# Transposes of a fused linear-attention and rational-activation MLP kernel by DMA instead of TensorE, with the queues, the stores, the start and the end rearranged

## The chip, the cores and the metric

The kernel runs on one core of a Trainium2 chip. The metric is the device time of one execution in microseconds (us), the median of several. The engines are named PE (TensorE matrix products) and PEld (its weight loads), DVE (VectorE), ACT (ScalarE), POOL (GpSimd) and SP (SyncE, which here only issues DMAs). Accumulators of TensorE lie in PSUM, everything else on the chip in SBUF. 16 DMA engines move data for all queues.

## The reference

```python
# attention: q, k, v, f_logit have shape (4, 8, 768, 48): batch, heads, time, head dimension
f = 1.0 / (1.0 + np.exp(-f_logit))
for t in range(S):
    state = f[:, :, t, :, None] * state + np.einsum('bhd,bhe->bhde', k[:, :, t], v[:, :, t])
    y[:, :, t] = np.einsum('bhd,bhde->bhe', q[:, :, t], state)
x = y.transpose(0, 2, 1, 3).reshape(3072, 384)
# MLP with a rational activation: w_in is (384, 2048), w_out (2048, 384)
h = x @ w_in
P = a[0] + a[1] * h + a[2] * h2 + a[3] * h3
Q = 1.0 + np.abs(b[0]) * np.abs(h) + np.abs(b[1]) * h2
return (P / (Q + 1e-06)) @ w_out
```

## The kernel before

The 3072 tokens are cut into 12 units of 256. A unit is loaded (`fn`, `kn`, `qn`, `vn`), its decays are summed and exponentiated (`cs`, `A0`, `A1`), multiplied into q and k (`qkp`), and transposed (`qkT`), because the scores `sc` contract over the head dimension. Masked scores and states give `y`, which ACT copies to `xT`. Each unit then has two groups of the MLP (24 groups in all): first-layer products `hp`, the numerator in `t`, the denominator's polynomial in `z`, a logarithm and an exponential (`lq`, `qi`) in place of a division, `gall = t * qi`, and the output products. The order of all instructions is fixed by a list of 654 tokens such as `T:4` (transposes of unit 4) or `Ub:11` (polynomial sum of group 23).

```python
def a_T(n, ps=ALL):                       # 16 transposes on TensorE, into PSUM
    ...
    for b in range(UB):
        for i in range(2):
            for p in range(npairs(ps)):
                nc.tensor.transpose(tp[:, b, i, p, :], s["qk"][:, i, ps.start + p, b].rearrange("t i d -> t (i d)"), ident)

def a_Te(n, ps=ALL):                      # and the copy out of PSUM, on ACT or VectorE
    copy(te_engine(n), t.rearrange(...), s["tp", 0].rearrange(...))

def m_add_u(n):                           # z += h: a DMA that adds, in GpSimd's queue, or VectorE
    ...
    if n in U_BY_DMA:
        nc.gpsimd.dma_start(out=s["u"], in_=s["h2"], accum_op=ALU.add)
    else:
        nc.vector.tensor_add(s["u"], s["z"], s["h2"])

def m_oe(m, b, eng, queue=None):          # copy of an output tile, and at once its store in SP's queue
    ...
    copy(eng, osb, ops.pop((m, b)))
    ...
    (queue or nc.sync).dma_start(out=dst[:, b, :], in_=osb)

# in the loop over the tokens: once unit n has read its inputs, those of unit n + 3 are loaded (SP's queue)
        if key in ("efl", "mq", "mk"):
            read[n] = read.get(n, 0) + 1
            if read[n] == 3 and n + 3 < NUN:
                load(n + 3)
```

Of the kernel before, what the change touches and what calls it, by code (L numbers as in the profile page):

```python
# [18 lines left out]
    efl-:0 efl:0 cs-:0 A0-:0 A1-:0 cs:0 A1:0 mk-:0 A0:0 mq-:0 T-:0 mk:0 mq:0 Te-:0 T:0 sc0:0 sv:0 Te:0  # L19
    efl:1 m0:0 al:0 sc1:0 st:0 cs:1 A0:1 m1:0 y-:0 mq:1 y:0 A1:1 mk:1 sw:0 su:0 xe:0 T:1 Te:1 ha0:0  # L20
    Ya0:0 ha1:0 sc0:1 sv:1 m0:1 Ya1:0 vl:3 al:1 st:1 sc1:1 za:0 efl:2 qa:0 cs:2 A1:2 ta:0 Ua:0 m1:1 sa:0
    hb0:0 sw:1 Ba:0 y:1 mk:2 A0:2 hb1:0 La0:0 Pa:0 Yb0:0 Ea:0 su:1 xe:1 mq:2 Yb1:0 T:2 ga:0 ha1:1 Te:2
    Ya1:1 ha0:1 zb:0 qb:0 Ya0:1 tb:0 Ub:0 Lb0:0 sc0:2 m0:2 Bb:0 hb0:1 sv:2 Ba:1 sc1:2 hb1:1 al:2 za:1
    m1:2 oa0:0 st:2 sw:2 Yb0:1 Eb:0 y:2 Yb1:1 qa:1 efl:3 sb:0 cs:3 xe:2 tb:1 A1:3 ta:1 Pb:0 ha1:2 A0:3
    zb:1 Ya1:2 gb:0 mq:3 ha0:2 Ya0:2 su:2 efl:4 qb:1 Bb:1 hb1:2 Yb1:2 oa1:0 Ua:1 Oa:0 cs:4 mk:3 T:3 Ub:1
    ta:2 La0:1 ob0:0 ob1:0 sa:1 sv:3 vl:4 Te:3 A1:4 sc0:3 qa:2 Ea:1 Ob:0 A0:4 efl:5 hb0:2 mk:4 m0:3
    sc1:3 mq:4 al:3 vl:5 m1:3 cs:5 st:3 sw:3 Lb0:1 sb:1 A0:5 y:3 za:2 Yb0:2 Pb:1 ua1:2 A1:5 qb:2 xe:3
    Eb:1 ua0:2 La1:2 su:3 T:4 sv:4 Pa:1 zb:2 La0:2 ga:1 Ub:2 ha0:3 Te:4 Ba:2 al:4 ha1:3 sc0:4 tb:2 mk:5
    gb:1 m0:4 Ya0:3 sa:2 efl:6 st:4 mq:5 vl:6 oa0:1 Bb:2 Ya1:3 Ea:2 oa1:1 sc1:4 hb1:3 sb:2 m1:4 sw:4
    Yb1:3 hb0:3 Oa:1 cs:6 Yb0:3 ob0:1 A0:6 y:4 za:3 qb:3 Pa:2 A1:6 ob1:1 qa:3 Lb0:2 ta:3 xe:4 su:4 T:5  # L30
    ha0:4 sa:3 zb:3 sv:5 Pb:2 Ba:3 ha1:4 ga:2 tb:3 Eb:2 Bb:3 Te:5 Ob:1 sc0:5 oa0:2 Ya0:4 efl:7 Ua:3 gb:2
    m0:5 mq:6 Ub:3 al:5 Pa:3 st:5 Ya1:4 oa1:2 Oa:2 hb0:4 sc1:5 La0:3 mk:6 Yb0:4 ob0:2 Ea:3 sw:5 sb:3
    vl:7 m1:5 hb1:4 ta:4 Yb1:4 cs:7 Lb0:3 qa:4 za:4 y:5 Ua:4 ob1:2 Ba:4 xe:5 T:6 sa:4 qb:4 zb:4 A1:7
    ha1:5 A0:7 su:5 sv:6 mq:7 Te:6 sc0:6 Pb:3 Ya1:5 Ob:2 ga:3 m0:6 Ub:4 ha0:5 sc1:6 al:6 st:6 Eb:3 oa0:3
    La0:4 hb0:5 Ya0:5 tb:4 m1:6 y:6 Ea:4 Pa:4 vl:8 sb:4 Bb:4 gb:3 za:5 sw:6 xe:6 mk:7 qa:5 oa1:3 Yb0:5
    Oa:3 hb1:5 ta:5 su:6 Ba:5 sa:5 T:7 Te:7 sv:7 ha1:6 efl:8 Yb1:5 ga:4 al:7 Lb0:4 Ya1:6 tb:5 cs:8 A0:8
    sc0:7 ob0:3 st:7 ob1:3 m0:7 zb:5 A1:8 ua1:5 sc1:7 Pb:4 sw:7 qb:5 m1:7 Eb:4 La1:5 ha0:6 gb:4 Ya0:6
    ua0:5 Ob:3 y:7 hb1:6 mq:8 efl:9 Bb:5 sb:5 mk:8 La0:5 xe:7 Pa:5 cs:9 Yb1:6 A0:9 T:8 Ub:5 ta:6 za:6
    oa0:4 Ea:5 Ba:6 qa:6 su:7 hb0:6 oa1:4 Te:8 A1:9 Yb0:6 ha1:7 sa:6 Lb0:5 ga:5 vl:9 ha0:7 Ya1:7 Oa:4
    sc0:8 Pb:5 tb:6 zb:6 sv:8 qb:6 ob0:4 m0:8 Pa:6 ua1:6 Ya0:7 al:8 Eb:5 mk:9 ua0:6 La1:6 st:8 La0:6  # L40
    sc1:8 ob1:4 sb:6 Bb:6 m1:8 Ba:7 za:7 sv:9 Ub:6 efl:10 hb0:7 Ea:6 y:8 hb1:7 Yb0:7 xe:8 gb:5 mq:9 Pb:6
    ha0:8 vl:10 Ob:4 qa:7 al:9 T:9 ta:7 Ua:7 Yb1:7 st:9 Bb:7 Lb0:6 ha1:8 Ya0:8 oa0:5 qb:7 Ya1:8 Te:9
    zb:7 oa1:5 Eb:6 Oa:5 cs:10 efl:11 ga:6 A0:10 A1:10 sa:7 sc0:9 Pa:7 hb0:8 tb:7 ob0:5 m0:9 sc1:9 gb:6
    ta:8 Yb0:8 mq:10 m1:9 ob1:5 hb1:8 La0:7 ub1:7 Ba:8 mk:10 qa:8 Yb1:8 y:9 Ob:5 za:8 Ea:7 Lb1:7 sb:7
    xe:9 vl:11 ga:7 ub0:7 tb:8 Lb0:7 Ua:8 zb:8 oa0:6 qb:8 cs:11 A1:11 T:10 A0:11 Pb:7 Te:10 Eb:7 Ub:8
    oa1:6 ha1:9 Oa:6 sa:8 sv:10 sc0:10 al:10 ha0:9 La0:8 st:10 mk:11 m0:10 Ya1:9 ob0:6 Ya0:9 Ea:8 ob1:6
    sc1:10 Pa:8 Lb0:8 sb:8 hb1:9 Bb:8 Ob:6 m1:10 hb0:9 Yb0:9 za:9 qa:9 sv:11 y:10 gb:7 ta:9 Yb1:9 xe:10
    mq:11 Ba:9 Eb:8 oa0:7 qb:9 Pb:8 al:11 T:11 Ua:9 zb:9 sa:9 Te:11 oa1:7 ga:8 ha0:10 Oa:7 sc0:11 tb:9
    La0:9 Ub:9 ha1:10 st:11 ob0:7 m0:11 sc1:11 Ya1:10 Ya0:10 Pa:9 Bb:9 ob1:7 Ea:9 sb:9 m1:11 hb0:10 Ob:7
    Lb0:9 hb1:10 za:10 qa:10 y:11 gb:8 Pb:9 Ua:10 Yb0:10 oa0:8 oa1:8 ta:10 Yb1:10 Ba:10 xe:11 Eb:9 Oa:8  # L50
    La0:10 sa:10 ha0:11 ha1:11 zb:10 qb:10 ob0:8 ga:9 Pa:10 Ub:10 tb:10 ob1:8 Bb:10 Ya0:11 sb:10 Ya1:11
    Pb:10 Ea:10 gb:9 za:11 hb1:11 Ob:8 Yb1:11 hb0:11 qa:11 Yb0:11 ta:11 Ba:11 oa0:9 sa:11 Ua:11 Lb0:10
    oa1:9 qb:11 zb:11 Oa:9 ob0:9 ga:10 tb:11 Ub:11 Eb:10 La0:11 ob1:9 Ea:11 Pa:11 Ob:9 gb:10 Lb0:11
    ob0:10 oa0:10 sb:11 Bb:11 ob1:10 Eb:11 ga:11 oa1:10 Oa:10 oa0:11 Pb:11 ob0:11 gb:11 ob1:11 oa1:11
    Oa:11 Ob:10 Ob:11
# [3 lines left out]
P_BY_DMA = {4, 5, 6, 7, 8, 9, 10, 11, 12, 13, 14, 15, 16, 17, 18, 19, 20, 21}  # L59

U_BY_DMA = {2, 3, 5, 6, 7, 8, 9, 11, 13, 14, 16, 17, 18, 19, 20, 21, 22, 23}

TE_ON_ACT = {1, 2, 4, 5, 6, 11}
O_ON_DVE = {(0, 1), (11, 1), (10, 1), (2, 0), (9, 1)}
# [3 lines left out]
def kernel(  # L68
# [74 lines left out]
    hold = w_pool.tile([1, 4, 16], BF16, name="hold")  # L143
# [6 lines left out]
    NUN = len(units)  # L150
    at_ = {}
# [3 lines left out]
    def load(n):  # L155
        c, u = units[n]
        at_[n] = dict(qk=qkp[n % NQK], ls=lsp[n % NQK], st=states[u], c=c, u=u)
        for name, src in (("fn", f_logit), ("kn", k), ("qn", q)):
            at_[n][name] = ld.tile([C, H, UB, D], F32, name=name)
            if n > 0:  # L160
                nc.sync.dma_start(out=at_[n][name].rearrange("p h b d -> p h (b d)"), in_=rows(src, n))
        if n == 0:
            for ps in HALVES:
                for name, src in (("fn", f_logit), ("kn", k), ("qn", q)):
                    for i in range(2):
                        hs = slice(HP * i + ps.start, HP * i + ps.stop)
                        nc.sync.dma_start(out=at_[n][name][:, hs].rearrange("t h b d -> t h (b d)"),
                                          in_=rows(src, n)[:, hs])

    def load_v(n):  # L170
        at_[n]["vn"] = vz[n % NV]
        for cc in range(UB):
            w = slice(CH * cc, CH * cc + CH)
            nc.gpsimd.dma_start(out=vz[n % NV][w, :, cc].rearrange("p h b d -> p h (b d)"), in_=rows(v, n)[w])  # L174

# [59 lines left out]
    def a_T(n, ps=ALL):  # L235

        s = at_[n]
        pool, tag = (psr, "r") if ps is HALVES[1] else (psA, "A")
        tp = pool.tile([P, UB, 2, npairs(ps), C], BF16, name="tp", tag=tag)
        for b in range(UB):  # L240
            for i in range(2):
                for p in range(npairs(ps)):
                    nc.tensor.transpose(tp[:, b, i, p, :],  # L243
                                        s["qk"][:, i, ps.start + p, b].rearrange("t i d -> t (i d)"),
                                        ident)
        s["tp", ps.start] = tp

# [3 lines left out]
    def a_Te(n, ps=ALL):  # L251
        s = at_[n]
        t = tile_at(s, "qkT", [P, UB, 2, HP, C], BF16)
        if ps is ALL:
            copy(te_engine(n), t.rearrange("p j a b c -> p (j a b c)"),
                 s["tp", 0].rearrange("p j a b c -> p (j a b c)"))
        else:
            copy(te_engine(n), t[:, :, :, ps].rearrange("p j a b c -> p (j a) (b c)"),
                 s["tp", ps.start].rearrange("p j a b c -> p (j a) (b c)"))
# [29 lines left out]
    def a_sc(n, half):  # L289
# [3 lines left out]
        for q_ in range(2):  # L293
            p = half * 2 + q_
            for b in range(UB):
                for i in range(2):
                    for cc in range(UB):
                        r, w = slice(64 * i, 64 * i + D), slice(CH * cc, CH * cc + CH)
                        nc.tensor.matmul(sc[w, i, q_, b, :], s["qkT"][r, b, 1, p, w], qcols(s, r, p, w),  # L299
# [7 lines left out]
    def qcols(s, r, p, w):  # L307
        return s["qkT"][r, :, 0, p, w]
# [10 lines left out]
    def a_y(n, ps=ALL):  # L319
# [7 lines left out]
        def clear(kk, r):  # L327
# [28 lines left out]
        if ps.start == 0:  # L356
            for kk in (0, KD - 1):
                clear(kk, slice(0, P))
        product(True, [(1, 1)])
        product(False, [(1, 1)])  # L360
        for i in range(2):
            if ps.start == 0:
                clear(0, slice(64 * i + 32, 64 * i + 48))
            if ps.stop == HP:
                clear(KD - 1, slice(64 * i, 64 * i + 16))
# [46 lines left out]

    def m_y(n, half):
        nc.scalar.copy(part_of(tile_of(n, "y"), half), mg[n]["hp", half].rearrange("p a n -> p (a n)"))  # L414

    def m_sq(n):
        s = mg[n]
        s["h2"] = ms.tile([P, W], BF16, name="h2")
        nc.vector.tensor_mul(s["h2"], s["y"], s["y"])  # L419

    def m_abs(n):
        s = mg[n]
        s["z"] = ms.tile([P, W], BF16, name="z")
        nc.vector.tensor_scalar(s["z"].bitcast(U16), s["y"].bitcast(U16), 0x7FFF, None,  # L424
# [21 lines left out]
    def m_ln(n, half):  # L446
        s = mg[n]
        lq = tile_of(n, "lq", F32, bufs=1)
        whole = "u" in s
        nc.scalar.activation(lq if whole else part_of(lq, half),  # L450
                             s["u"] if whole else s["u", half].rearrange("p a n -> p (a n)"),
                             AF.Ln, scale=sig[:, 2:3], bias=1.0 + 1e-6)
# [5 lines left out]

    def m_t(n):
# [211 lines left out]
```

## Time and profile before

| what | before |
|---|---|
| median time | 233.1 us at first, 233.3 beside the changed kernel, 233.5 in the later rounds |
| span in the profile | 231.3 us |
| copies into `xT` start at | 20.72 us (unit 0), then 35.84, 48.99, 68.59 ... 197.16 (unit 11) |
| last `xT` to the end | 34.1 us |

### The profile page before, as it was taken

What the parts mean: (1) busy time and instruction counts of PE and PEld (TensorE: products, weight loads), DVE (VectorE), ACT (ScalarE), POOL (GpSimd) and SP (SyncE); (2) the same over time, 40 slices, a digit from 0 to 9 for tenths busy, and PEclk for the clock granted to TensorE, in tenths of its full rate; (3) what the DMA queues carried; (4) which work ended last, traced back from release to release, by engine and by line L of the source; (5) the groups of instructions that cost most, each with busy time, mean ns of one, the idle gap of its engine ahead of it and who ended that gap; (6) DMA issues with size and microseconds to landing.
All of it is one profiled execution on the core that took longest, in us unless ns stands there. A gap on an engine that the chain in (4) does not pass through costs nothing.

```text
span 231.3 us, 7110 instructions
## 1 busy us (share of the span) xinstructions
PE 211.0 (91%) x3106; PEld 150.1 (65%) x3106; DVE 212.1 (92%) x257; ACT 202.1 (87%) x202; POOL 66.3 (29%) x91
## 2 busy tenths in 40 slices
PE   7299797979989999999999999999999999997981
PEld 3166565767657767676776775876677878764540
DVE  5686599999999999999999999999999999999950
ACT  4424889997999999999999999999998999799950
POOL 8360860023305126035112411424132122313000
PEclk9959979999979999999999999999999999999998
DMA  7999999999999999999999999876599969998502
GB/s 108 261 144 202 186 188 199 222 250 258 197 272 262 187 222 206 183 272 194 185 202 247 192 261 203 131 140 125 74 181 212 203 120 205 188 213 198 127 34 102
DMA packets 63054, 43.71 MB, mean 189 GB/s; under 512 B 51760, under 2 KB 58416, under 8 KB 63024
## 3 DMA queue, kind: packets, MB, share of 16 engines
q0 software_dynamic: 21632, 24.38, 65.9%
q1 hardware_dynamic: 41104, 18.88, 32.7%
q8 instruction: 24, 0.39, 0.7%
q10 hardware_dynamic: 288, 0.00, 0.1%
q14 instruction: 6, 0.05, 0.1%
HBM read 25.17 MB, written 4.72 MB: 129 GB/s over the span
## 4 chain that ended last, share of the span: by engine, by line
DVE 58%; PE 21%; issue 10%; DMA 6%; ACT 3%; SPq 1%; POOL 0%; DVEq 0%; POOLq 0%; ACTq 0%
DVE scm L315 8%; DVE h L419 8%; DVE gall L485 8%; DVE t L465 7%; PE op L502 7%; PE hp L400 6%; DVE t L460 5%; DVE qkp L232 5%; DVE pb L468 5%; DVE z L424 4%; DVE qkT L249 2%; PE y L352 2%; DMA z<-h 2%; DVE t L476 2%; DVE state L381 2%
## 5 line engine op out<-in xcount | busy, mean ns | idle before, releaser
L400 PE MATMUL hp<-xT,w_in_sb 128*128 128x256 bf16 x576 | 70.2, 275 | 0.6 <-ACT y L414 0.2
L502 PE MATMUL op<-w_out_sb,gall 128*128 128x384 bf16 x368 | 65.5, 326 | 2.4 <-ACT osb L249 1.7
L400 PEld LDWEIGHTS <-w_in_sb 128*128 128x128 bf16 x576 | 55.1, 99 | 11.1 <-issue 2.0
L502 PEld LDWEIGHTS <-gall 128*128 128x128 bf16 x384 | 36.1, 98 | 26.4 <-issue 2.2
L414 ACT CAST y<-hp 128x1024 bf16<-128x1024 f32 x48 | 48.0, 1024 | 1.7 <-PE hp L400 0.9
L455 ACT ACTIVATE qi<-lq 128x2048 bf16<-128x2048 f32 x24 | 46.4, 1934 | 0.1
L450 ACT ACTIVATE lq<-z,sig 128x2048 f32<-128x2048 bf16 x20 | 40.4, 2020 | 2.9 <-DMA z<-h 2.8
L442 POOL DMA_DIRECT2D z<-h x18 | 17.1, 949 | 88.5 <-DVE z L424 38.4
L315 DVE TENSOR_TENSOR scm<-sc,mask 128x1024 bf16<-128x1024 f32 x24 | 29.1, 1213 | 4.2 <-PE sc L299 4.2
L474 POOL DMA_DIRECT2D t<-pb x18 | 17.5, 975 | 45.7 <-DVE t L465 30.1
L485 DVE TENSOR_TENSOR gall<-t,qi 128x2048 bf16<-128x2048 bf16 x24 | 29.1, 1211 | 1.0 <-ACT qi L455 1.0
L465 DVE TENSOR_TENSOR t<-t,h 128x2048 bf16<-128x2048 bf16 x24 | 29.1, 1211 | 0.0
L419 DVE TENSOR_TENSOR h<-y 128x2048 bf16<-128x2048 bf16 x24 | 29.0, 1211 | 0.0
L226 ACT ACTIVATE A<-cs 128x768 f32<-128x768 f32 (+1 forms) x26 | 18.7, 767 | 4.2 <-PE cs L217 4.1
L174 POOL DMA_DIRECT2D vz<-in_v_dram x24 | 21.8, 1131 | 0.3 <-POOL vz L531 0.3
L460 DVE TENSOR_SCALAR t<-y,a_sb 128x2048 bf16<-128x2048 bf16 x24 | 19.4, 811 | 0.5
L468 DVE TENSOR_SCALAR pb<-y,a_sb 128x2048 bf16<-128x2048 bf16 x24 | 19.4, 811 | 0.0
L424 DVE TENSOR_SCALAR z<-y 128x2048 uint16<-128x2048 uint16 x24 | 16.5, 688 | 0.5 <-ACT lq L450 0.4
L217 PE MATMUL cs<-lsp,U 128*128 128x384 bf16 (+1 forms) x39 | 10.9, 341 | 6.2 <-ACT lsp L204 6.1
L243 PE MATMUL tp<-ident,qkp 128*128 128x128 bf16 x192 | 13.8, 227 | 2.6 <-DVE qkp L232 2.4
L243 PEld LDWEIGHTS <-qkp 128*128 128x128 bf16 x192 | 12.2, 101 | 5.5 <-DVE qkp L232 3.5
L352 PE MATMUL y<-scm,vz 128*32 128x128 bf16 (+1 forms) x768 | 15.4, 228 | 0.0
(75 smaller groups left out, 253.7 us busy)
## 6 DMA issues: line engine op xcount, KB each, us to landing
z<-h POOLq DMA_DIRECT2D x18, 512.0 KB, 6.2
t<-pb POOLq DMA_DIRECT2D x18, 512.0 KB, 6.6
out_dram<-osb SPq DMA_DIRECT2D x24, 192.0 KB, 4.1
fn<-in_f_logit_dram SPq DMA_DIRECT2D x11, 384.0 KB, 5.9
kn<-in_k_dram SPq DMA_DIRECT2D x11, 384.0 KB, 6.1
qn<-in_q_dram SPq DMA_DIRECT2D x11, 384.0 KB, 6.9
vz<-in_v_dram POOLq DMA_DIRECT2D x24, 96.0 KB, 6.4
w_in_sb<-in_moe_w_in_dram POOLq DMA_DIRECT2D x8, 192.0 KB, 5.1
```

The costliest lines, as they stand in the source:

```text
L243: nc.tensor.transpose(tp[:, b, i, p, :], s["qk"][:, i, ps.start + p, b].rearrange("t i d -> t (i d)"), ident)
L315: nc.vector.tensor_mul(m.rearrange("s i q b t -> s (i q) (b t)"), s["sc", half].rearrange("s i q b t -> s (i q) (b t)"), mb)
L400: nc.tensor.matmul(hp[:, e, :], w_in_sb[:, kk, f * P:(f + 1) * P], xT[:, kk, :], start=(kk == 0), stop=(kk == KD - 1))
L414: nc.scalar.copy(part_of(tile_of(n, "y"), half), mg[n]["hp", half].rearrange("p a n -> p (a n)"))
L419: nc.vector.tensor_mul(s["h2"], s["y"], s["y"])
L450: nc.scalar.activation(lq if whole else part_of(lq, half), s["u"] if whole else s["u", half].rearrange("p a n -> p (a n)"), AF.Ln, scale=s ...
L455: nc.scalar.activation(part_of(tile_of(n, "qi"), part, parts), part_of(mg[n]["lq"], part, parts), AF.Exp, scale=-1.0)
L460: nc.vector.tensor_scalar(tile_of(n, "t", bufs=3), mg[n]["y"], a_sb[:, 3:4], a_sb[:, 2:3], op0=ALU.mult, op1=ALU.add)
L465: nc.vector.tensor_mul(s["t"], s["t"], s["h2"])
L468: nc.vector.tensor_scalar(tile_of(n, "pb"), mg[n]["y"], a_sb[:, 1:2], a_sb[:, 0:1], op0=ALU.mult, op1=ALU.add)
L485: nc.vector.tensor_mul(galls[m][:, lo:lo + w, :].rearrange("p a n -> p (a n)"), part_of(s["t"], part, parts), part_of(s["qi"], part, parts))
L502: nc.tensor.matmul(ops[m, b], galls[m][:, mm, b * C:(b + 1) * C], w_out_sb[:, mm, :], start=(mm == 0), stop=(mm == KF - 1))
```

## The change

Its intent: take the transposes of units 3 to 11 and their copies off the three full engines and give them to the DMA engines. SP issues the DMA transposes, so its queue is kept for transposes and stores, and the loads of units 6 to 11 go into GpSimd's queue, which so far held the weights, v and the adding DMAs. Stores become tokens of their own (`Da`, `Db`). Besides, the affine steps of two groups are merged (`t2`, `B2`), seven adding DMAs go back to engines, the first unit's loads are reordered over three queues, the loads of unit 3 wait behind the weights, and the last group runs in halves.

```diff
-P_BY_DMA = {4, 5, ..., 21}            # 18 groups
-U_BY_DMA = {2, 3, 5, ..., 23}         # 18 groups
+P_BY_DMA = {4, 6, 8, ..., 22}         # 15 groups
+U_BY_DMA = {3, 5, 8, ..., 22}         # 14 groups
...
+    FIRST_BY_DMA = 3
...
+            for name, src in (("fn", f_logit), ("kn", k), ("qn", q)):   # unit 0
+                for ps in HALVES:
...
+                        act = i == 1 and ps is HALVES[0]
+                        (nc.gpsimd if name == "qn" else nc.scalar if act else nc.sync).dma_start(
...
+        if n >= FIRST_BY_DMA:
+            nc.sync.dma_start(out=qkT(s).rearrange("f i p b t -> f (i p b) t"),
+                              in_=s["qk"].rearrange("t i p b h d -> t (i p b h d)"), transpose=True)
+            return
...
+    def m_store(m, b):
+        nc.sync.dma_start(out=dst[:, b, :], in_=ops.pop((m, b)))
...
+        "fl": lambda n: load(n, queue=nc.gpsimd),
+    steps["t2"] = lambda n: affine(both(n, "t"), both(n, "y"), 2)
+    steps["B2"] = lambda n: affine(both(n, "y"), both(n, "y"), 0)
... (the list of tokens is a new one)
-            if read[n] == 3 and n + 3 < NUN:
-                load(n + 3)
+        if key == "T" and n in (1, 2):
+            load(n + 3)
```

## The prediction

> **What bounds the kernel now.** I read the page first (busy shares, the 40 slices), then the chain that ended last, then windows of 10 and 20 us, then the groups by shape, and last the timelines of the first 36 and final 30 us. The page:
>
> ```profile
> PE 211.0 (91%) x3106; PEld 150.1 (65%) x3106; DVE 212.1 (92%) x257; ACT 202.1 (87%) x202; POOL 66.3 (29%) x91
> ...
> PE   7299797979989999999999999999999999997981
> ...
> DVE  5686599999999999999999999999999999999950
> ACT  4424889997999999999999999999998999799950
> ...
> DMA  7999999999999999999999999876599969998502
> ...
> DVE 58%; PE 21%; issue 10%; DMA 6%; ACT 3%; SPq 1%; POOL 0%; DVEq 0%; POOLq 0%; ACTq 0%
> ```
>
> No engine stands alone: three of them work 87 to 92% of the span. The holes are at the two ends (VectorE's 5, 6, 8, 6, 5 at the start, the 5 and 0 at the end). The chain is VectorE 58%, and listed in order of time it runs on VectorE almost alone up to 172 us, then on TensorE from 173 to 205 us, then through a DMA to the end. The windows say the same (columns: PE, weight loads, DVE, ACT, POOL busy us, clock, DMA share, GB/s):
>
> ```profile
> 20.00:30.00 10.00, 8.25 (x141) 5.83 (x130) 5.59 (x9) 6.51 (x8) 6.02 (x10) 0.91 1.20 200
> 40.00:60.00 20.00, 18.54 (x265) 13.66 (x263) 20.00 (x24) 18.66 (x20) 5.44 (x6) 1.00 1.11 237
> 140.00:160.00 20.00, 20.00 (x303) 14.34 (x302) 20.00 (x23) 19.65 (x21) 7.12 (x8) 1.00 0.76 143
> ```
>
> Until about 120 us VectorE has no idle time while TensorE has some; later both are full. TensorE's true load comes from rates, not busy time: the timeline has 24 first-layer products in 2.78 us, so (2.78 - 0.27)/23 = 0.109 us each, and 16 second-layer products in 2.76 us, 0.163 us each. Per unit of work that is 48 x 0.109 + 32 x 0.163 = 10.4 us; from the chain's TensorE stretch the rest of a unit adds 0.89 us (16 transposes), about 1.9 (y), 0.7 (sc), 0.75 (sv), 0.7 (cs) and on average 0.6 (u): 16.0 us. The copies into xT start at 20.7 us (first unit) and 197.2 us (twelfth): 16.05 us a unit. So TensorE is as much the bound as VectorE.
>
> The end of the program is a chain of single steps:
>
> ```profile
> 205.02 2.78 PE L400 MATMUL hp<-xT,w_in_sb 128*128 128x256 bf16 x24 [0.19 <-ACT y L414]
> ...
> 212.82 0.86 POOL L442 DMA_DIRECT2D z<-h  x1 [3.50 <-DVE z L424]
> ...
> 218.42 2.01 ACT L450 ACTIVATE lq<-z,sig 128x2048 f32<-128x2048 bf16 x1 [0.47 <-DMA z<-h]
> ...
> 222.40 1.23 DVE L485 TENSOR_TENSOR gall<-t,qi 128x2048 bf16<-128x2048 bf16 x1 [1.04 <-ACT qi L455]
> ```
>
> The last adding DMA takes 212.8 to 218.3 us, and ln, exp, gall, output products and the store follow it, whole tile after whole tile, to 231.3.
>
> **What the Trainium skill says.** (1) "TensorE: Matmul & The Clock Gate", Part 4: PE-mode transpose: such a transpose ends in PSUM, so a copy must follow. The trace agrees: 16 transposes and then a copy of 1.88 us on ACT or 1.21 us on VectorE. (2) "DMA: Bandwidth & Descriptors", DMA Transpose (X-bar): 2-byte data, into SBUF, from SP or ACT only; that is why the SP queue is cleared for them. Its section Latency and other measured facts gives 261 GB/s for one with a non-contiguous middle dimension; this trace has none, so my estimate is 0.52 MB / 261 GB/s = 2.0 us moving time. (3) "VectorE: DVE Perf Modes", The perf-mode tier table: bf16 tensor_scalar at 4 elements a cycle, 693 ns for 2048. The trace has 688 ns for z but 811 ns where the two scalars are columns (t, pb). (4) The DMA page, Issuing engines are not separate DMA queues: moving loads to another issuer gives no bandwidth, only issue time and order. Here the queues differ in what stands ahead in them, and I expect that to be the gain.
>
> **The change, part by part.** The instruction order of both kernels gives the counts, these rows the durations:
>
> ```profile
> L249 ACT COPY qkT<-tp 128x2048 bf16<-128x2048 bf16 x6 | 11.3, 1879 | 1.6 <-PE tp L243 1.6
> L249 DVE COPY qkT<-tp 128x2048 bf16<-128x2048 bf16 x5 | 6.0, 1209 | 0.0
> L468 DVE TENSOR_SCALAR pb<-y,a_sb 128x2048 bf16<-128x2048 bf16 x24 | 19.4, 811 | 0.0
> L476 DVE TENSOR_TENSOR t<-t,pb 128x2048 bf16<-128x2048 bf16 x6 | 7.3, 1210 | 0.0
> ```
>
> *Transposes.* Units 3 to 11 go by DMA: TensorE loses 144 of 192 transposes, 144 x 0.055 = 7.9 us. ACT's qkT copies go from 6 to 1: 5 x 1.88 = -9.4 us. VectorE's whole copies go from 5 to 1: 4 x 1.21 = -4.8.
>
> *Merged affine steps.* t and pb were 48 instructions of 2048. Now 19 are of 4096 and 10 of 2048. At 4 elements a cycle (0.96 GHz, by the skill) 2048 take 0.53 us; the chain has them 0.72 us apart, so a merge saves the fixed 0.19: 19 x 0.19 = -3.6 us.
>
> *Adding DMAs.* 36 become 29. t+pb on VectorE goes from 6 to 9: 3 x 1.21 = +3.6 us. z+h on VectorE stays at 2, but is now for a middle group and the very last one. The identity-matmul form goes from 4 groups to 8: 32 more matmuls of 512 columns at 512/2.4 GHz = 0.213 us, +6.8 us of TensorE; ACT then reads lq's source in 1024-wide halves: -5 x 2.02 + 8 x 1.11 + 2 x about 1.16 = +1.1.
>
> *Sums.* VectorE: -4.8 -3.6 +3.6 -0.5 (one osb) +3.7 (five memsets moved from POOL to it, at the start) -2.3 (the mask casts, which occupied 3.97 to 8.09 us, become four) = -3.9, so about 208 us busy. ACT: -9.4 +1.1 +0.5 (osb) +0.2 = -7.6, about 194.5. TensorE: -7.9 +6.8 = -1.1 in all, but unevenly: units 6 to 11 lose 6 x 0.89 = 5.3 us and one group of u matmuls (1.7), while the early units gain five groups (8.6) and lose 2.7. So relief falls where TensorE is the bound (after 120 us), and load where it has room. POOL: 7 fewer accumulates (-6.7), memsets -3.7, 18 whole loads at perhaps 2 us (estimate: a v load of half as many rows took 1.13) +36, small q loads +2: about 94 us, no bound.
>
> *On the path.* Start: ACT stood 3.02 us for the second half of fn, which SP had issued behind kn and qn; now both halves go first and qn goes through POOL. Also the first-layer products of unit 0 come ahead of unit 1's transposes, which should shrink VectorE's 3.85 us wait for sc at 25.7 us. I take 4 us. Middle: of TensorE's 7 us relief after 120 us and VectorE's saving there (some 4.5 of copies, half the merges, less the added sums) I take 4, and 0 before 120 us, where the sums nearly cancel. End: group 23 adds on VectorE (1.2 us in place of 5.5) and runs ln, exp, gall and the last products in halves. From the last first-layer product (207.8) to the end took 23.5 us; unhindered the new steps need about 0.95 + 3.0 + 2.2 + 2.0 + 0.6 + 1.3 + 1.1 + 3.8 = 15. But VectorE and ACT were busy with other groups until 222 us, so I take 3. Against it I put 3 us for new waits on transposes and for POOL's accumulates standing behind loads. Sum: -4 -4 -3 +3 = -8, from 233.1 to 225.
>
> **Rivals.**
> *The DMA engines become the bound.* For: the share digits are 9 nearly everywhere and the landing times (6.2 us for 0.5 MB) show queueing. q0 holds 65.9% of 16 engines; by bytes 18.9 of its 24.4 MB are accumulates, so 0.659 x 231.3 x 18.9/24.4 / 36 = 3.3 us of all engines each. Seven fewer free 23 us, nine transposes at 2 us cost 18. Against: it nearly cancels. If a transpose takes 6 us or more of the engines, +54 - 23 = +31 us on a system with some 10% free, and the kernel would end at 233 to 240.
> *Head of line in a queue.* A transpose feeds the scores on TensorE's path; if it lands late, TensorE, VectorE and ACT all stand. For: one issuing queue, stores in it, and the scores of a unit follow its products closely. Against: products for the next unit are made most of a unit (16 us) ahead and stores are placed as late steps. If five of nine units lose 2 us each: about 232.
> *The slack is smaller or larger than I took.* TensorE's 16 us a unit hardly changes in sum (-0.1), so if it is the bound everywhere only start and end gain: 227 to 229. If the early third, where engines waited on each other, tightens to VectorE's 17 us less the savings, and the tail takes all its 8 us: 217 to 219.
>
> **Range and chances.** The work removed and the shorter ends are certain, the DMA latency is not, and the error on each of the four terms is about 2 to 3 us: 225, with 219 to 231 for 8 in 10. Faster by over 2% means under 228.5: 0.76. Within 2%: 0.17. Slower: 0.07.
>
> **What would show it.** Right: qkT copies gone from ACT (about 194.5 us busy), VectorE near 208, transposes landing in 4 to 8 us with TensorE waiting under 3 us in all on qkT, first products on VectorE before 8 us rather than at 10.3, xT 15 to 15.5 us apart after 120 us, the last 23.5 us shrunk to about 17. Wrong: TensorE standing for qkT several times, landing times of accumulates grown from 6.2 towards 10 us, ln waiting for z again and again, or VectorE's zero idle time replaced by waits on DMA.

## More of the kernel before

For the comparison, three lines more are needed, of the page's DMA issues: tile written and read, queue, how many, size of each, and the median us from issue to landing.

```profile
z<-h POOLq DMA_DIRECT2D x18, 512.0 KB, 6.2
t<-pb POOLq DMA_DIRECT2D x18, 512.0 KB, 6.6
fn<-in_f_logit_dram SPq DMA_DIRECT2D x11, 384.0 KB, 5.9
```

These are the transfers that share the DMA engines with anything that the change adds: 36 adding DMAs and the loads. They land in about 6 us.

## The result, and the profile after

The changed kernel took 263.1 us (median of four, 262.1 to 267.6) beside 233.3 us of the kernel before; both are correct. The ratio is 1.125, with a 95% interval of 1.121 to 1.130. Ratios here are the mean time of one kernel's fast runs over that of the other's of the same rounds, so not quite the ratio of the medians quoted. The profiled run was itself the slowest (267.6 us, span 265.8 us, marked slow), so times inside it are some 2% long (its other three runs took 262.1 to 263.8 us; "slow" marks a run over 1.5% above the fastest of its kernel). No cause below is argued from a difference as small as that.

The page of the changed kernel: busy shares, slices of PE, VectorE and the DMA engines, two queues, and the chain that ended last, by engine and then by line (its heaviest lines are the first of the second row).

```profile
PE 216.9 (82%) x2994; PEld 149.3 (56%) x3004; DVE 208.3 (78%) x238; ACT 195.9 (74%) x204; POOL 75.6 (28%) x101
...
PE   6896899791699935079978999985999988999884
...
DVE  7666699992599980056969999994789989899971
...
DMA  6998999999349999960599998999999999879813
...
q0 software_dynamic: 22832, 28.19, 62.9%
q1 hardware_dynamic: 39504, 15.93, 33.1%
...
DMA 35%; PE 20%; DVE 16%; issue 12%; ACT 10%; POOL 6%; SPq 0%; ACTq 0%; POOLq 0%; DVEq 0%
```

The work that the engines do shrank just as counted: VectorE 208.3 us against 208 predicted, ACT 195.9 against 194.5. TensorE's busy time alone did not: it rose from 211.0 to 216.9 us where a fall of 1 was counted, with fewer matmuls, at a mean clock of 0.92 of full speed against 0.97 before. Yet the time grew by 30 us, so nearly all of that is idle time. Where VectorE had an unbroken row of nines it now has holes, above all two zeros in the middle. The chain, which was 58% VectorE and 6% DMA, is 35% DMA. In order of time, its longest pieces are these (start, us, what):

```profile
56.14 12.85 DMA qkT<-qkp
...
84.01 30.72 DMA qkT<-qkp
...
128.61 10.97 DMA t<-y
```

A transpose of 30.7 us stands on the chain. The waits (engine, line, what it waited for: us in total, times, the longest) and the landing times of the nine transposes and of the others say the same:

```profile
DVE scm L338 <- PE sc L322: 38.4, 11, 16.6
...
PE sc L322 <- DMA qkT<-qkp: 25.0, 4, 11.2
```

```profile
DMA to landing us min/median/max: 4.2/10.7/30.7
```

```profile
z<-h POOLq DMA_DIRECT2D x14, 512.0 KB, 5.9
...
fn<-in_f_logit_dram POOLq DMA_DIRECT2D x6, 384.0 KB, 11.1
```

TensorE stood 25 us for `qkT` and VectorE 38 us for the scores behind it. The worst stretch, in windows of 4 us (columns as in the prediction: PE, weight loads, DVE, ACT, POOL, clock, DMA share, GB/s):

```profile
88.00:92.00 4.00, 4.00 (x79) 2.98 (x80) 4.00 (x5) 3.98 (x6) 2.68 (x3) 1.00 1.28 228
...
96.00:100.00 4.00, 2.50 (x8) 1.23 (x10) 2.88 (x5) 2.33 (x2) 0.00 (x0) 0.50 1.55 77
...
108.00:112.00 4.00, 0.00 (x0) 0.00 (x0) 0.00 (x0) 0.00 (x0) 0.00 (x0) 0.50 1.26 119
```

Look at the last two columns. (A share over 1 means that the times of the packets add up to more than the window on 16 engines.) In the second line the DMA share is higher than in the first, while the rate falls from 228 to 77 GB/s; in the third it is about as high as in the first, at 119 GB/s: the DMA engines are occupied, but move little. Meanwhile every engine stops, and TensorE comes back at half its clock (0.50 in the window from 112 us, 0.54 in that from 116, 1.00 from 120).

The copies into `xT` date the loss. Against the kernel before, the changed one is at these units (us, from the timelines of ACT):

```
unit      0      1      2      3      4      5      6      7      8      9     10     11
before  20.72  35.84  48.99  68.59  85.93 101.80 113.67 129.78 148.36 166.87 182.82 197.16
after   16.71  36.10  55.81  77.00  94.51 125.41 147.09 163.22 175.81 199.31 214.72 233.40
lag     -4.0   +0.3   +6.8   +8.4   +8.6  +23.6  +33.4  +33.4  +27.5  +32.4  +31.9  +36.2
```

The start is won as predicted and lost again by unit 1. Most of the loss, 25 us, falls on units 5 and 6, whose transposes took 30.7 and 18.0 us to land. The lag of 6.8 us at unit 2 is not the transposes' doing, since the first of them is issued at 56.14 us; f1 below, which has none, shows it too and makes it good by unit 3.

### The profile page after: what moved, and what is told of

Read it like the earlier page. It is cut to its first block, busy times and chain, and to the rows that moved or that the text cites. A ratio compares the mean times of both kernels' runs of the same rounds, so it can differ in the third digit from the quotient of the medians.

```text
span 265.8 us, 6884 instructions
## 1 busy us (share of the span) xinstructions
PE 216.9 (82%) x2994; PEld 149.3 (56%) x3004; DVE 208.3 (78%) x238; ACT 195.9 (74%) x204; POOL 75.6 (28%) x101
## 3 DMA queue, kind: packets, MB, share of 16 engines
q1 hardware_dynamic: 39504, 15.93, 33.1%
## 4 chain that ended last, share of the span: by engine, by line
DMA 35%; PE 20%; DVE 16%; issue 12%; ACT 10%; POOL 6%; SPq 0%; ACTq 0%; POOLq 0%; DVEq 0%
DMA qkT<-qkp 16%; PE hp L423 10%; DMA t<-y 7%; DMA z<-h 6%; PE op L535 4%; DVE t L500 3%; ACT y L449 3%; ACT qi L489 2%; DMA qn<-in_q_dram 2%; DVE h L454 2%; DMA w_in_sb<-in_moe_w_in_dram 2%; DVE gall L518 2%; DVE scm L338 2%; DVE t L494 1%; POOL vz L184 1%
## 5 line engine op out<-in xcount | busy, mean ns | idle before, releaser
L423 PE MATMUL hp<-xT,w_in_sb 128*128 128x256 bf16 x576 | 75.9, 288 | 4.1 <-ACT y L449 2.8
L338 DVE TENSOR_TENSOR scm<-sc,mask 128x1024 bf16<-128x1024 f32 x24 | 29.3, 1221 | 38.4 <-PE sc L322 38.4
L489 ACT ACTIVATE qi<-lq 128x2048 bf16<-128x2048 f32 (+1 forms) x25 | 46.2, 1849 | 0.1
L486 ACT ACTIVATE lq<-z,sig 128x2048 f32<-128x2048 bf16 (+1 forms) x17 | 32.4, 1910 | 2.0 <-DMA z<-h 2.0
L322 PE MATMUL sc<-qkT 48*64 48x128 bf16 x384 | 10.9, 237 | 26.9 <-DMA qkT<-qkp 25.0
L518 DVE TENSOR_TENSOR gall<-t,qi 128x2048 bf16<-128x2048 bf16 (+1 forms) x25 | 29.3, 1175 | 3.8 <-DMA t<-y 2.2
L507 POOL DMA_DIRECT2D t<-y x15 | 15.4, 1030 | 37.6 <-DVE y L494 15.2
L322 PEld LDWEIGHTS <-qkT 48*64 48x64 bf16 x384 | 6.8, 114 | 32.7 <-DMA qkT<-qkp 25.9
L486 ACT ACTIVATE lq<-u,sig 128x1024 f32<-128x1024 f32 x16 | 17.8, 1119 | 4.7 <-PE u L469 4.5
L494 DVE TENSOR_SCALAR y<-y,a_sb 128x4096 bf16<-128x4096 bf16 (+1 forms) x15 | 17.1, 1138 | 0.2
L494 DVE TENSOR_SCALAR t<-y,a_sb 128x4096 bf16<-128x4096 bf16 (+1 forms) x14 | 16.6, 1188 | 0.7 <-ACT y L449 0.7
L375 PE MATMUL y<-scm,vz 128*32 128x128 bf16 (+1 forms) x768 | 14.6, 220 | 0.0
(76 smaller groups left out, 265.8 us busy)
```

What stands on the lines that cost most here:

```text
L338: nc.vector.tensor_mul(m.rearrange("s i q b t -> s (i q) (b t)"), s["sc", half].rearrange("s i q b t -> s (i q) (b t)"), mb)
L423: nc.tensor.matmul(hp[:, e, :], w_in_sb[:, kk, f * P:(f + 1) * P], xT[:, kk, :], start=(kk == 0), stop=(kk == KD - 1))
L486: nc.scalar.activation(lq if whole else part_of(lq, half), u, AF.Ln, scale=sig[:, 2:3], bias=1.0 + 1e-6)
L489: nc.scalar.activation(part_of(tile_of(n, "qi"), part, parts), part_of(mg[n]["lq"], part, parts), AF.Exp, scale=-1.0)
L494: nc.vector.tensor_scalar(out, y, a_sb[:, c + 1:c + 2], a_sb[:, c:c + 1], op0=ALU.mult, op1=ALU.add)
L518: nc.vector.tensor_mul(galls[m][:, lo:lo + w, :].rearrange("p a n -> p (a n)"), part_of(one(n, "t"), part, parts), part_of(s["qi"], part, ...
```

## The experiments

My theory after the result: a DMA transpose costs the DMA engines more than my 2 us, and slows whatever is in flight beside it. The rivals: the new order of instructions or the new queue of the loads is the cause, or the plain number of small packets is. Twelve kernels were run.

### e1: the changed kernel with all transposes on TensorE

```diff
-    FIRST_BY_DMA = 3
+    FIRST_BY_DMA = 12
+            if key == "T" and 3 <= n < FIRST_BY_DMA:
+                later.append(n)      # run as soon as no scores or y stand in that PSUM slot
... (then a_T and a_Te of that unit)
```

A direct swap would have had the transposes of a unit wait for a PSUM slot held by scores of the unit before, in an order that can't end, so they are deferred to the next free moment.

> The changed kernel with all twelve units transposed on TensorE (as soon as the PSUM slot is free) and copied by ACT or VectorE; everything else as changed. Theory A (the DMA transposes cost the time, by landing late and by slowing the other transfers): 230 to 242 us, no TensorE wait for a transfer into qkT. Theory B (the new order, the sets of adding DMAs and the load queue are at fault, the transposes only show it): above 252 us.

Measured: 248.3 us (247.1 to 250.0), ratio 1.064 (1.058 to 1.070), correct. So with the transposes back on TensorE about half of the 30 us goes. The other half e1 leaves open: TensorE has its 144 transposes again (213.5 us busy) and ACT the copies (204.5), in an order that was made for a kernel without them. VectorE has no stop in the middle as after the change, but seven slices of five to eight tenths between start and end: small waits, spread out.

### e2: units 3 to 6 on TensorE, 7 to 11 by DMA

```diff
-    FIRST_BY_DMA = 3
+    FIRST_BY_DMA = 7
... (deferral as in e1)
```

> The same with units 3 to 6 on TensorE and 7 to 11 by DMA. Theory A, if it is the transposes that meet bursts of loads (units 3, 5 and 6): 238 to 247 us, the two long waits of 8 and 11 us gone. If every transpose costs alike: about 250. Theory B: above 255 us.

Measured: 249.8 us, ratio 1.069 (1.062 to 1.075), correct. The late transposes cost about nothing against TensorE ones, since the interval overlaps that of e1. TensorE waited 6.7 us for `qkT` in all, and the transposes landed in 7.2 us (median). What separates the changed kernel from e1 is units 3 to 6.

### b1, b2, b3: nine unread transfers put into the kernel before

The same bytes (0.52 MB of `qkp` a unit, units 3 to 11) go to a tile that nobody reads, from SP's queue, in the unchanged order: as a transpose (b1), as a plain copy (b2), and as a copy cut into pieces of 256 bytes, the size of a transpose's packets (b3).

```diff
+        if key == "T" and n >= 3:
+            dead = at.tile([P, 2 * HP * UB, C], BF16, name="dead", bufs=2)
+            nc.sync.dma_start(out=dead, in_=at_[n]["qk"].rearrange("t i p b h d -> t (i p b h d)"), transpose=True)   # b1
+            nc.sync.dma_start(out=dead.rearrange("p a c -> p (a c)"), in_=at_[n]["qk"].rearrange(...))                # b2
+            # b3: the tile's last dimension is C + 32, so that the pieces do not join
            nc.sync.dma_start(out=dead[:, :, 0:C], in_=at_[n]["qk"].rearrange("t i p b h d -> t (i p b) (h d)"))      # b3
```

> The kernel before with nine additional DMA transposes (units 3 to 11, into a tile that nobody reads), issued by SP where the TensorE transposes of the unit are issued. If transposes in flight slow the other transfers: 238 to 250 us, landing times of loads and of adding DMAs above 8 us. If only the wait for their result costs: within 3 us of before (233).

> The same with nine plain copies of the same bytes, same queue and places. If it is the bytes that cost: equal to the dead transposes. If it is the transposing: within 3 us of before (233 to 236).

> The kernel before with nine unread plain copies of the same bytes, cut into 256-byte pieces as the transposes are (some 2048 packets each). If the number of packets costs: 255 to 270 us, as with the dead transposes (267). If it is the transposing: 235 to 241 us, as with the plain copies of whole rows (237).

Measured: b1 267.2 us (261.0 to 270.7; only its fastest run counts as fast, so there is no ratio), b2 237.2 us (ratio 1.013, 1.005 to 1.020), b3 240.1 us (1.028, 1.024 to 1.033). All are correct. Nine transposes that nobody reads cost at least 27 us. The same bytes copied cost some 3 (the ratio is of fast runs; one of b2's four is slow), and the same bytes in the same small pieces 6.6. So it is neither the bytes nor the number of packets, but the transposing. The queue of SP's and ACT's transfers (packets, MB, share of 16 engines' span) before, in b1, b2 and b3:

```profile
q1 hardware_dynamic: 41104, 18.88, 32.7%
```
```profile
q1 hardware_dynamic: 59824, 23.60, 49.5%
```
```profile
q1 hardware_dynamic: 42400, 23.60, 37.4%
```
```profile
q1 hardware_dynamic: 59680, 23.60, 41.9%
```

With the spans of 231.3, 265.6, 236.2 and 238.4 us, the added occupation of all 16 engines is (0.495 x 265.6 - 0.327 x 231.3)/9 = 6.2 us for a transpose, and in the same way 1.4 us for a copy and 2.7 us for a copy in small pieces. (Of the 6.2 us the transpose's own packets are 5.9, as counted below; the rest is in other packets of that queue.) In b1 the engines wait for the transfers beside the transposes, and for the tile that a slow one still reads (so "unread" does not mean that nothing waits for it):

```profile
PE tp L243 <- DVE qkp L232: 17.2, 4, 10.3
DVE pb L468 <- DMA t<-pb: 15.9, 4, 13.8
...
DVE qkp L232 <- DMA dead<-qkp: 10.3, 2, 7.3
```

The records of single packets in the traces tell more than the shares. I took all packets of 256 bytes of that queue (18432 in each kernel, 2048 for one transfer) and asked how long each took.

```
                        median ns   95% under   over 100 ns   their share of the time   sum/16 engines, each
after (transposes)          18          93          904               43%                     5.0 us
b1 (transposes)             18          79          724               51%                     5.9 us
b3 (plain, same size)       18          31            2                0%                     2.7 us
```

The usual packet of a transpose took just as long as one of a copy. But one in 20 to 25 stood for 0.1 us up to 3 us, and in the copies only two did. By stretches of time, with what else was moved meanwhile in the trace of the changed kernel:

```
transpose of unit        mean ns a packet   sum/16, each   moved beside it (KB)
4, 10, 11                      22            2.8 to 2.9 us  almost nothing (0 to 73)
7                              25               3.2 us      adding DMAs 512, v 50
3                              37               4.7 us      whole loads 1015, v 16
8, 9                         42, 48           5.4, 6.1 us   v 181 and 246, stores 42 and 43
5 and 6 together               66               8.4 us      whole loads 1811, v 192
```

Alone, a transpose costs 2.8 us of the engines, in company up to 8.4. In b3 nine copies of the same pieces, beside adding DMAs, v, loads and stores alike, took 19 to 25 ns a packet throughout. What inside the chip makes a transpose's packets stand I can't see from here. That company brings it on is what the stretches have in common, with unit 7 as the exception that had company and did not suffer. Its company was nearly all adding DMAs, and e2's trace has the same: unit 7 beside 560 KB of them took 3.2 us, unit 9 beside v (221 KB) and stores (72 KB) 6.7. But b1's last transpose took 4.5 us beside 156 KB of adding DMAs alone, so which company matters is not settled.

One rival stays untested: SP itself. Issuing one transpose held SP for 1.9 to 9.6 us in b1 (median 6.0), where a copy held it for 0.5 to 2.9 in b2 and 0.6 to 4.9 in b3 (medians 1.3 and 1.4), and b1's loads and stores stand behind it in that queue. No run tells whether the long issue is a cause or itself waits for the DMA engines. It can't be the whole, since the adding DMAs, which GpSimd issues, landed later too: 7.9 and 9.3 us in b1 (z and t, medians) against 6.9 and 7.4 in b3.

### f1, f2: the changed kernel with stale `qkT`

f1 issues no transpose, and the scores of units 3 to 11 read the `qkT` of unit 1 or 2. The result is wrong (relative error 0.03). f2 issues the nine transposes into a tile that nobody reads.

```diff
+        if s["n"] >= FIRST_BY_DMA:
+            s = at_[1 + s["n"] % 2]                 # qkT(s) of an early unit
...
...
-            nc.sync.dma_start(out=qkT(s)..., transpose=True)
+            nc.sync.dma_start(out=dead, in_=s["qk"].rearrange("t i p b h d -> t (i p b h d)"), transpose=True)   # f2 alone
```

> Wrong result on purpose: the changed kernel without the nine DMA transposes; units 3 to 11 read the transposed tiles of units 1 and 2. It shows what the new order does when transposing costs nothing. If the prediction's sum for the engines holds and only the transfers failed: 219 to 226 us. If the order itself loses (first case without transposes on TensorE, which was 248): above 235 us.

> Wrong result on purpose: as before, but the nine transposes are issued into a tile that nobody reads. Its excess over the run without them is what transposes cost by slowing other transfers; what is missing up to 263 us is the wait for their result. If the slowing is the main part, as the dead transposes in the kernel before suggest (+34 us): 245 to 258 us. If the wait is: below 235 us.

Measured: f1 229.4 us (228.3 to 230.3), ratio 0.982 (0.977 to 0.988). f2 had 241.0 us once, and 250.9, 251.8 and 261.5 in runs that are over 1.5% above that, so it has no ratio; its median is 251.3 us.

f1 gives the value of everything else in the change, with transposes for nothing and never late: 4 us. So the order of instructions is by itself no cause of the loss. VectorE has its row of nines again, with one seven in it:

```profile
PE   6698679979899899999989999999989999999791
...
DVE  7766689999999999999999999999799999999880
```

The copies into `xT` of f1, and how far those of the changed kernel lie behind them (its profiled run was the slowest, f1's the fastest, so some 6 us of the last figure are scatter):

```
unit           0      1      2      3      4      5      6      7      8      9     10     11
f1         17.47  34.54  54.22  66.21  84.58  96.03 114.31 130.46 143.08 160.28 176.61 193.47
behind it   -0.8   +1.6   +1.6  +10.8   +9.9  +29.4  +32.8  +32.8  +32.7  +39.0  +38.1  +39.9
```

The steps stand at units 3, 5, 6 and 9, whose transposes landed after 12.8, 30.7, 18.0 and 10.7 us.

f2 puts about 22 us on top of f1 (12 to 32 by single runs) although nobody reads what is transposed, so that part comes from slowing other transfers, or from holding SP's queue. The first is seen in the packets: those of the loads in GpSimd's queue took 27 us of all engines in f1 and 36 in f2, those of v 28 and 34. First f1, then f2, issues to landing:

```profile
z<-h POOLq DMA_DIRECT2D x14, 512.0 KB, 5.6
out_dram<-osb SPq DMA_DIRECT2D x24, 192.0 KB, 3.7
...
fn<-in_f_logit_dram POOLq DMA_DIRECT2D x6, 384.0 KB, 9.9
```
```profile
z<-h POOLq DMA_DIRECT2D x14, 512.0 KB, 8.4
out_dram<-osb SPq DMA_DIRECT2D x24, 192.0 KB, 7.9
...
fn<-in_f_logit_dram POOLq DMA_DIRECT2D x6, 384.0 KB, 15.1
```

The profiled runs of b1 (267.4 us) and f2 (251.8) are marked slow, but the one fast run of each still lies above its partner: 27.5 us above the kernel before, 11.5 above f1. The remaining 12 us to 263 are then what waiting for the transposes themselves adds. How the two share the total is only as sure as f2's scatter allows.

### b4, g1, g2: the queue of the loads

b4 is the kernel before with the loads of units 6 to 11 in GpSimd's queue. g1 is the changed kernel, and g2 is e1, with these loads back in SP's queue.

```diff
-                load(n + 3)
+                load(n + 3, nc.gpsimd if n + 3 >= 6 else nc.sync)       # b4, in the kernel before
...
-        "fl": lambda n: load(n, queue=nc.gpsimd),
+        "fl": load,                                                     # g1 and g2
```

> The kernel before with the loads of units 6 to 11 issued by GpSimd in the queue of the adding DMAs, nothing else. If this part of the change is harmless: 232 to 236 us. If loads ahead of the adding DMAs in one queue, or loads waiting behind them, cost part of the 15 us that the changed kernel keeps without its transposes: 238 to 246 us.

> The changed kernel with the loads of units 6 to 11 back in the SP queue, at the same steps; transposes by DMA stay. Theory (the transposing itself costs): the queue of the loads hardly matters, 257 to 266 us, perhaps with longer waits for qkT because loads stand ahead of a transpose. Rival (the queue of the loads is what slows it, as in b4, where they held up the adding DMAs): 240 to 250 us.

> e1 (all transposes on TensorE in the changed kernel, 248.3 us) with the loads of units 6 to 11 back in the SP queue. Theory: e1's remaining distance to 233 is its order of instructions, which is made for DMA transposes and does not fit TensorE ones; the queue gives little: 244 to 250 us. Rival: the loads in GpSimd's queue hold up the adding DMAs there: 234 to 240 us.

Measured: b4 248.1 us (ratio 1.061, 1.054 to 1.069), g1 262.0 us (1.110, 1.103 to 1.116), g2 249.3 us (1.067, 1.063 to 1.072), all correct. b4's loads stand at the head of GpSimd's queue until their buffer is free, and the adding DMAs behind them start late. Its waits:

```profile
POOL kn L161 <- DVE qkp L232: 31.1, 5, 12.4
...
ACT lq L450 <- DMA z<-h: 12.7, 5, 7.4
```

So the queue can cost 14.6 us. The changed kernel escapes that, since it issues these loads at tokens of their own, placed after the buffer is free. In g1 and g2 the queue then matters little. g2's interval overlaps that of e1. Two of g1's four runs are slow (263.3 and 263.7); its fast ones (257.6 and 260.7) are 1.4% faster than the fast runs of the changed kernel, some 4 us. g1 is telling in another way. Its transposes landed in 5.7 us (median) in place of 10.7, and TensorE waited 10.9 us for `qkT` in place of 25.0 (in the fastest run of g1 and the slowest of the changed kernel, 10 us apart), yet most of the 30 us stays. The stop has moved to an adding DMA:

```profile
ACT y L449 <- DMA t<-y: 21.8, 3, 18.0
DVE gall L518 <- DMA t<-y: 16.1, 1, 16.1
```

The transpose of unit 7 there took 25.7 us to land beside two adding DMAs, v and stores, and its packets took 112 ns in the mean. Clearing one collision made room for another.

### v1, v2: what of the change is worth having

v1 is the kernel before with the changed start alone (loads of unit 0 over three queues in the order fn, kn, qn, masks first on GpSimd, memsets on VectorE, the mask in four casts). v2 has the changed end besides (group 23 added on VectorE, its last steps in halves).

```diff
+                        act = i == 1 and ps is HALVES[0]
+                        (nc.gpsimd if name == "qn" else nc.scalar if act else nc.sync).dma_start(     # v1 and v2
...
-U_BY_DMA = {2, 3, 5, ..., 22, 23}
+U_BY_DMA = {2, 3, 5, ..., 22}                                                                       # v2 alone
-Lb0:11 ... Eb:11 ga:11 ... gb:11 ob1:11 oa1:11
+Lb0:11 Lb1:11 ... Eb-:11 Eb:11 ga:11 ... gb-:11 ob1-:11 oa1-:11 gb:11 oa1:11 Oa:11 ob1:11              # v2 alone
```

> The kernel before with the changed start alone (order and queues of the first unit's loads, masks first on GpSimd, memsets moved to VectorE, mask in four casts); steps, transposes, stores and later loads as before. Theory: the start is a real gain of up to 4 us that the changed kernel won in its first unit (its first xT at 16.7 us against 20.7) and lost later to the DMA engines, so here it should stay: 229 to 231 us. Rival: what follows is set by the weights' loads and by VectorE from about 30 us, and the gain is taken back by unit 2: 232 to 234 us.

> v1 and the changed end besides: group 23 added on VectorE, and its ln, exp, gall and last output products in halves. Theory: the two shorter ends can be had without DMA transposes; the end gives the 3 us of the prediction: 226 to 229 us. Rival: VectorE and ACT are busy with other groups until the end, as in the changed kernel whose last stretch stayed at 22 us: within 1 us of v1.

Measured: v1 231.7 us (ratio 0.993, 0.990 to 0.996), v2 231.9 us (0.993, 0.990 to 0.996), both correct. v1 beats the kernel before, though by less than 1%. Its first `xT` comes at 18.84 us (1.9 us earlier) and its last at 196.01 (1.15 us earlier). That is less than the 4 us of the changed kernel's first unit, but it stays, and v1's 231.7 lies between the 229 to 231 of the theory and the 232 to 234 of the rival: neither range was met. The end is worth nothing, as the rival said. The timeline of v2 shows why (start, us, what; in brackets the wait before it):

```profile
219.13 6.26 PE L510 MATMUL op<-w_out_sb,gall 128*128 128x384 bf16 x36
...
221.85 1.29 DVE L493 TENSOR_TENSOR gall<-t,qi 128x1024 bf16<-128x1024 bf16 x2
...
225.42 0.48 ACT L258 COPY osb<-op 128x384 f32<-128x384 f32 x1 [3.75 <-PE op L510]
```

Both halves are worked out between 221.85 and 223.14 us, but TensorE is working through output products without a gap from 219.13 to 225.39. The last copy waits for these, as it did before.

## Why the prediction was wrong, point by point

The prediction was 225 us, with 219 to 231; it came to 263. Its chance for slower by over 2% was 0.07.

*The step that failed* is the first rival's sentence "Seven fewer free 23 us, nine transposes at 2 us cost 18. Against: it nearly cancels", and its estimate "0.52 MB / 261 GB/s = 2.0 us moving time". The freed side was right in size: the packets of adding DMAs, of 4096 bytes, took 101.9 us of all engines before and 80.7 after, 21 us less (2.8 us each, where the prediction had worked out 3.3). The other side was mis-sized: the nine transposes took 44.6 us (9 x 5.0), not 18. A lone one took 2.8 us, and those that had company took up to 8.4. The rival even had a figure for this, +31 us of DMA work from transposes of 6 us, but turned it into 233 to 240, as if it could be shared out over the free 10%. It came in lumps: two transposes met six loads, and VectorE stood for 16.6 us at one go.

*The term "+3 us for new waits on transposes and for POOL's accumulates standing behind loads"* should have been about 34: the changed kernel's 263.1 less f1's 229.4. The part on accumulates behind loads hardly appears, since the loads' tokens come late enough, though b4 shows what it could have cost.

*"Here the queues differ in what stands ahead in them, and I expect that to be the gain"*: no gain was found. Moving the loads cost 14.6 us in b4, and moving them back in the changed kernel (g1) gave some 4 us by its two fast runs.

*Start, -4*: right for the first unit (16.71 us against 20.72, and the first product on VectorE at 6.95 us, before the 8 us I named). Of this f1 kept 3.2 us at its first unit and v1 1.9. In v1's time 1.8 us remained.

*Middle, -4*: right for its late half, wrong in sum. With transposes for nothing, f1's `xT` are (193.47 - 17.47)/11 = 16.0 us apart, as before (16.04). From unit 6 (at 114 us in both) to unit 11 f1 took 79.2 us against 83.5, so the 4 us after 120 us came, at 15.8 us a unit. But from unit 0 to unit 6 it took 96.8 against 93.0, where the prediction put 0. The order of the whole list is new there, and the count itself had more work for TensorE in the early groups (+8.6); that this is the reason is not shown.

*End, -3*: wrong. From the last `xT` to the end it took 34.1 us before and 33.1 in f1. v2 shows the limit, TensorE's output products, which the step "1.3 + 1.1 + 3.8" of my sum took as if only the last group's were left.

*The counts of work* were right: ACT 195.9 us against 194.5, VectorE 208.3 against 208. A merged affine step of 4096 took 1.34 to 1.35 us against 1.345 worked out (twice 0.53 and the fixed part). TensorE's count (-1.1) is the exception: 211.0 us busy became 216.9 with the stops, at the lower clock, and 205.5 in f1. POOL had 75.6, not 94, since issuing a whole load took it about 1.2 us, not 2.

*The signs I named* for being wrong were two of the right ones: TensorE stood for `qkT` four times (25.0 us), and VectorE got waits where it had had none. But I named waits on DMA, and these were for the scores (38.4 us) one step behind. The landing times of the adding DMAs, which I had named too, did not grow in the median (5.9 us for z, against 6.2 before), though one of them is on the chain with 11 us. They grew in f2 (8.4 us against f1's 5.6), where engines wait only 1.8 us for the transposes.

The Trainium skill bears on this in two places. Its page "Advanced Engine Details and Errata", section X-Bar Transpose (TRN2), says "TRN2 transpose DMAs are as fast as regular DMAs". The runs disagree: b1's transposes occupied the engines for 6.2 us each, where b2's plain copies of the same bytes took 1.4, and the times are 267 us against 237. The figure of 261 GB/s, in "DMA: Bandwidth & Descriptors", section Latency and other measured facts, is nearer to the lone transposes: 0.52 MB in 2.8 us is 187 GB/s. I used it for transposes that were not alone, and that was the mistake.

What stays open: why e1, with all transposes on TensorE, is at 248 us and not near 233. Its three full engines have 6 to 9 us more work each than f1's, and I take its order for the reason, which no run shows. It also stays open what company slows a transpose (that of unit 7 in the changed kernel, beside 512 KB of adding DMAs, was hardly slowed), and how much of the loss comes from the long issues that hold SP.

## What to carry to other kernels

Before moving work to the DMA engines, put the new transfers unread into the old kernel: it costs a few lines, and here it would have shown the 30 us before anything else was rearranged. Read the DMA share and the rate together, since a high share with a falling rate means that transfers stand, and then look at single packets, not at means. A transfer whose duration depends on its neighbours must not feed a step that three full engines wait for, unless it is issued far ahead or in a quiet moment, as the transposes of units 4, 10 and 11 were.

## What the Trainium skill lacked or had wrong

- "Advanced Engine Details and Errata", X-Bar Transpose (TRN2): transposes were not as fast as regular DMAs in a kernel with other traffic. 6.2 us of the 16 engines each against 1.4 us for a plain copy of the same bytes and 2.7 us for one in 256-byte pieces (b1, b2, b3).
- "DMA: Bandwidth & Descriptors", Rules for kernel authors: the rule that a transpose next to ordinary DMAs needs nothing held for the results (all kernels meant to be right were), but not for time. In company the packets of a transpose took 25 to 66 ns in the mean (112 in g1) against 22 alone, and other transfers were slowed too: the adding DMAs from 5.6 to 8.4 us, stores from 3.7 to 7.9 (f1, f2).
- The same page, Latency and other measured facts: one figure for a transpose's bandwidth can mislead. From issue to landing the nine took 4.2 to 30.7 us, and a lone one 2.8 us of the engines (187 GB/s).
- The same page, Issuing engines are not separate DMA queues: it says that issuing from several engines only saves the sequencer's time. The page has elsewhere that a DMA's wait happens on the issuing sequencer, but lacks what follows for the choice of issuer: a load which waits for its buffer holds up everything behind it in the issuer's queue. b4 lost 14.6 us to it.
- "VectorE: DVE Perf Modes", The perf-mode tier table: `tensor_scalar` has one figure for bf16 there. A multiplication and an addition with two column scalars took 811 ns for 2048 elements, a bitwise AND with one constant (on the same 16 bits as uint16) 688 ns. No run tells whether the columns or the second operation make the difference.
